# Order of the first four attention groups: scores behind the preceding group's transposes, maxima ahead of its normalisation, fewer fill matmuls

## The chip, the core and the metric

The kernel runs on one core of a Trainium2 chip. The metric is the time of one execution on the device, in microseconds (us). A core has five engines with in-order queues of their own: TensorE (PE in the profile; its weight loads are PEld), VectorE (DVE), ScalarE (ACT), GpSimd (POOL) and SyncE (SP), which here only issues DMA transfers. They wait for each other on semaphores.

## The reference, cut to what matters

A chunked attention with memory keys (4 batches, 8 heads, 768 queries, head size 64) is followed by two pairs of dense layers, all in fp32:

```python
for c in range(nc):                       # chunks of 32 queries
    scores = scale * q_c @ k_full.T       # 8 memory keys and the keys around the chunk
    a = exp(scores - max(scores))
    out_c = (a / (sum(a) + 1e-09)) @ v_full
x = out as (3072 tokens, 512)
h = x @ moe_w_in;  x = (h - tanh(h)) @ moe_w_out         # 512 -> 2048 -> 512
h = x @ moe2_w_in; x = piecewise(h) @ moe2_w_out         # the same sizes
```

The weights arrive as 64-bit floats, as pairs of 32-bit words, and the kernel itself rounds them to fp32.

## The kernel before

**Groups.** The attention is worked in 24 groups of 128 tokens (four chunks of 32). Four groups make one token block of 512, on which the first layer's matmuls run. Groups 0 to 3 are worked alone, ahead of everything else, in the loop `for j in range(PER)` near the end of the kernel; later groups are slipped in between the steps of the layers by tables of events. Instructions stand on each engine in the order in which the Python code issues them: nothing reorders them afterwards.

**One group.** `att_scores` is 64 small matmuls into PSUM (PE). `att_max` is a row maximum and its subtraction (DVE, two instructions of the latter). `att_exp` is one ACT instruction. `att_sum` is a sum, an addition and a reciprocal (DVE). `att_transpose` is 4 transposes of the exponentials (PE), `att_at` copies them to SBUF (ACT), `att_values` is 64 small matmuls with the values (PE), `att_norm` scales by the reciprocal (DVE), `att_x` is 4 transposes (PE). `att_xh` (ACT) and `att_xl` (DVE) split the result into a rounded part xh and a rest xl. Each fp32 product is made of three: xh with whi, xl with whi, xh with wlo.

**Weights.** A 512 KB tile of the first layer (raw_0, raw_1, ... in this text) is brought up in five steps: `round_act` (two ACT instructions), `round_mag` (two on DVE), `round_sign` (one on DVE, one on POOL), `split_weights_hi` (ACT, makes whi) and `split_weights_lo` (DVE, makes wlo). The tile is loaded into one of four staging buffers, so the load of raw_4 waits until POOL is done with raw_0, that of raw_5 for raw_1, and so on.

**The first layer.** `hidden(s)` is one step: 12 matmuls, 4 for each of the parts 0 (xh, whi), 1 (xl, whi) and 2 (xh, wlo). Step 0 is done in two pieces: the columns of groups 0 to 2 (384 columns) inside the loop of the first groups, the rest of group 3 behind it. Two PSUM buffers hold the steps, so `hidden(2)` waits until `gate(0)` (ACT, then DVE) has read step 0, and `hidden(3)` for `gate(1)`.

**Loads.** All of the start's loads stand on SP's queue in a fixed order: queries, keys, then a weight tile, then the values of each group. Each waits for the eighth one before it to land. None of the loads of groups 0 to 3 waits for an engine.

**Fills.** `warm(n, fill)` issues n matmuls on zeros whose result nobody reads. They stand in PE's queue in the pauses of the first groups: 6 behind the scores, 2 behind the transposes, 2 behind the values (`KEEP`).

Of the kernel before, what the change touches and what calls it, by code (L numbers as in the profile page):

```python
# [27 lines left out]
KEYS = NMEM + CTX  # L28
WIN = NMEM + LEFT + CHUNK + SEEN
NPAIR = H // 2  # L30
KC = DM // 128
FC = DFF // 128
NEG = -3.0e38
# [5 lines left out]
PER = 4  # L39
# [3 lines left out]


WARM = 11
KEEP = {"s": 6, "t": 2, "v": 2}

LAG = FC

# [29 lines left out]
def tile_memory_attention_two_mlps(  # L79
# [51 lines left out]
    def round_act(phase, which, fc, part=None, tag=None):  # L131
        stage = stage_t[phase, which, fc]
        low, high = stage[:, :, 0], stage[:, :, 1]
        if part != 1:
            t = slot(tag or (f"raw1_{fc % 3}" if which else f"raw0_{fc}"), f"raw{phase}{which}_{fc}")
            raw_t[phase, which, fc] = t

            nc.scalar.activation(out=t, in_=high.bitcast(F32), func=AF.Abs)
        if part != 0:

            nc.scalar.activation(out=low, in_=low.bitcast(U32), func=AF.Copy, scale=2.0 ** -29)
# [11 lines left out]
    def round_sign(phase, which, fc):  # L153
        stage = stage_t.pop((phase, which, fc))
        bits = raw_t[phase, which, fc].bitcast(I32)
        nc.vector.scalar_tensor_tensor(
            out=bits, in0=stage[:, :, 1], scalar=-0x40000000, in1=bits, op0=ALU.bitwise_and, op1=ALU.bitwise_or
        )

        eng = nc.vector if phase else nc.gpsimd  # L160
        eng.tensor_tensor(out=bits, in0=bits, in1=stage[:, :, 0], op=ALU.add)  # L161
# [7 lines left out]
    def split_weights_hi(s, which):  # L169
        phase, b, fc = steps[s]  # L170
        r = raw_t[phase, which, fc]
        hi = slot(f"whi{which}_{s % (W1O if which else 2)}", f"whi{which}_{s}", F32R)
        nc.scalar.activation(out=hi, in_=r, func=AF.Copy)  # L173
        split_t[s, which] = hi

    def split_weights_lo(s, which):
        phase, b, fc = steps[s]
        r, hi = raw_t[phase, which, fc], split_t[s, which]
        lo = slot(f"wlo{which}_{s % (W1O if which else 2)}", f"wlo{which}_{s}", F32R)
        nc.vector.tensor_tensor(out=lo, in0=r, in1=hi.bitcast(F32), op=ALU.subtract)  # L180
        split_t[s, which] = hi, lo
# [205 lines left out]
    def att_scores(t, pair):  # L387
        qt, kt = st[t]["q"], st[t]["k"]
        sp = pair[:, :, 4 * D:].rearrange("p c (a k) -> p c a k", a=NPAIR)
        for pr in range(NPAIR):  # L390
            for j in range(GC):
                for hh in range(2):
                    nc.tensor.matmul(  # L393
                        sp[j * CHUNK:(j + 1) * CHUNK, hh, pr, :],
                        qt[j][hh * D:(hh + 1) * D, pr, :],
                        kt[j][hh * D:(hh + 1) * D, pr, :],
                        start=True, stop=True,
                    )
        st[t]["sp"] = sp

    def att_max(t):

        e = slots.tile([128, 4, 2, WIN], F32, tag=f"e{t % 2}", name=f"e{t}")
        mx = att.tile([128, 2, NPAIR], F32, tag="mx", name=f"mx{t}")
        s = st[t]["sp"]

        if t % GPB == 0:
            nc.vector.memset(s[:CHUNK, :, :, NMEM:NMEM + LEFT], NEG)
        if t % GPB == GPB - 1:
            nc.vector.memset(s[128 - CHUNK:, :, :, WIN - SEEN:], NEG)  # L410
        nc.vector.tensor_reduce(out=mx, in_=s, op=ALU.max, axis=AX.X)
        st[t]["e"] = e
        if t in BY_HEAD:
            nc.vector.tensor_scalar(out=mx, in0=mx, scalar1=-scale, scalar2=None, op0=ALU.mult)
            st[t]["mx"] = mx
            return
        for hh in range(2):
            nc.vector.tensor_tensor(
                out=e.rearrange("p (b c) u k -> p c u b k", c=2)[:, hh],
                in0=s[:, hh].rearrange("p (u b) k -> p u b k", u=2),  # L420
                in1=mx[:, hh].rearrange("p (u b) -> p u b", u=2)[:, :, :, None].to_broadcast([128, 2, 2, WIN]),
                op=ALU.subtract,
            )

    def att_exp(t):
        e = st[t]["e"]
        if t not in BY_HEAD:
            nc.scalar.activation(out=e, in_=e, func=AF.Exp, scale=scale)
            return
        mx, s = st[t]["mx"], st[t]["sp"]  # L430
        st[t]["r"] = r = att.tile([128, 4, 2], F32, tag="r", name=f"r{t}")
        for g in range(4):
            for u in range(2):
                hh, pr = g % 2, 2 * u + g // 2
                nc.scalar.activation(
                    out=e[:, g, u, :], in_=s[:, hh, pr, :], func=AF.Exp, scale=scale,
                    bias=mx[:, hh, pr:pr + 1], accum_out=r[:, g, u:u + 1],
                )

    def att_sum(t):  # L440
        if t in BY_HEAD:
            r = st[t]["r"]
        else:
            r = att.tile([128, 4, 2], F32, tag="r", name=f"r{t}")
            nc.vector.tensor_reduce(out=r, in_=st[t]["e"], op=ALU.add, axis=AX.X)
        nc.vector.tensor_scalar(out=r, in0=r, scalar1=1e-9, scalar2=None, op0=ALU.add)
        nc.vector.reciprocal(out=r, in_=r)
        st[t]["r"] = r

    def att_transpose(t, p):  # L450
        e = st[t]["e"].rearrange("p g u k -> p g (u k)")
        for g in range(4):
            nc.tensor.transpose(p[:, g * GQ:(g + 1) * GQ], e[:, g, :], ident)  # L453
        st[t]["tp"] = p

    def att_at(t):
        at = slots.tile([128, 4, GQ], F32, tag=f"at{t % 2}", name=f"at{t}")
        nc.scalar.activation(out=at, in_=st[t]["tp"].rearrange("p (g c) -> p g c", g=4), func=AF.Copy)
        st[t]["at"] = at
# [35 lines left out]
    def att_xl(t):  # L495
        b, o = t // PER, t % PER * GQ
        xh, xl = x_tiles(0, b)
        nc.vector.tensor_tensor(  # L498
            out=xl[:, :, o:o + GQ], in0=st.pop(t)["xp"], in1=xh[:, :, o:o + GQ].bitcast(F32), op=ALU.subtract
        )  # L500
# [52 lines left out]
    def hidden(s, n0=0, n1=N, parts=range(3)):  # L553
        phase, b, fc = steps[s]
        xh, xl = x_tiles(phase, b)
        hi, lo = split_t[s, 0]
        if s not in h_t:
            h_t[s] = ps_h.tile([128, 512], F32, tag="h", name=f"h{s}")[:, :N]
        hp = h_t[s][:, n0:n1]
        for j in parts:  # L560
            w, x = ((hi, xh), (hi, xl), (lo, xh))[j]
            for kc in range(KC):
                nc.tensor.matmul(  # L563
                    hp, w[:, kc * 128:(kc + 1) * 128], x[:, kc, n0:n1],
                    start=j == 0 and kc == 0, stop=j == 2 and kc == KC - 1,
                )
# [471 lines left out]
    def warm(n, ps):  # L1038
        for _ in range(n):
            nc.tensor.matmul(ps, zeros[:, :128], zeros, start=True, stop=True)  # L1040
# [9 lines left out]
    load_weights(0, 0, PER - 1)  # L1050
    att_load(PER)

    def start_scores(j):
        pool, tag = ((ps_a, "a"), (ps_acc, "acc0"))[j % 2]
        st_pair[j] = pool.tile([128, 2, 512], F32, tag=tag, name=f"start_a{j}")
        att_scores(j, st_pair[j])

    start_scores(0)
    for j in range(PER):
        last = j == PER - 1  # L1060
        if not last:
            warm(KEEP["s"], fill)
        att_max(j)
        if j:
            att_xl(j - 1)
        if last:
            split_weights_lo(0, 0)
            hidden(0, 0, EARLY_N, (0,))
        if 1 < j:
            round_sign(0, 0, j - 2)  # L1070
        att_exp(j)
        att_sum(j)
        tx = ps_acc.tile([128, 2, 512], F32, tag="acc1", name=f"start_tx{j}")
        att_transpose(j, tx[:, 0, :])
        att_at(j)
        if j == 2:
            split_weights_hi(0, 0)
        if j:
            round_act(0, 0, j - 1)
        if last:  # L1080
            split_weights_hi(1, 0)
            hidden(0, 0, EARLY_N, (1,))
        else:
            warm(KEEP["t"], fill)
        att_values(j, st_pair.pop(j))
        if last:
            hidden(0, 0, EARLY_N, (2,))
        else:
            warm(KEEP["v"], fill)
            start_scores(j + 1)  # L1090
        att_norm(j)
        if last:
            split_weights_lo(1, 0)
        if j:
            round_mag(0, 0, j - 1)
        att_x(j, tx[:, 1, :])
        att_xh(j)
    att_xl(PER - 1)
    round_sign(0, 0, 2)
    round_act(0, 0, 3)  # L1100
    round_rest(0, 0, 3)
    for j in range(AHEAD):
# [105 lines left out]
```

## Time and profile before

| | |
|---|---|
| three runs | 1069.24, 1071.01 and 1071.11 us; median 1071.01 us |
| the profiled execution, first to last instruction | 1070.1 us (0.9 us under the median) |
| PE busy | 1052.4 us, 98% of the span |
| DVE, ACT, POOL busy | 855.7, 650.0 and 42.7 us |
| granted PE clock, mean | 0.997 |

No other time than its span is given for the profiled execution, so sums below are made against 1070.1 us and set on the median. A span counts from the first instruction to the last. "Busy" of PE is near the whole span, so what is left to win or to lose lies in the few stretches in which PE waits; nearly all of them are in the first 60 us, where the changed code stands.

### The profile page before, as it was taken

How to read it: one execution, taken by the hardware profiler on the slowest of the kernel's cores; microseconds unless marked ns; L12 is line 12 of the kernel's file. 1: busy time of each engine (PE TensorE's matmuls, PEld its weight loads, DVE VectorE, ACT ScalarE, POOL GpSimd, SP SyncE). 2: the span in 40 equal slices, each digit the busy share in tenths (PEclk: the TensorE clock that was granted, in tenths of full speed). 3: DMA queues.
4: the chain of work that ended last, by engine and by line, in shares of the span. 5: the costliest groups of instructions: out<-in, count | busy, mean ns of one | idle time of the engine just before them, and what ended most of it. 6: DMA issues, size and time to landing. Idle time of an engine off the chain costs nothing.

```text
span 1070.1 us, 21112 instructions
## 1 busy us (share of the span) xinstructions
PE 1052.4 (98%) x7589; PEld 859.7 (80%) x7589; DVE 855.7 (80%) x1511; ACT 650.0 (61%) x1203; POOL 42.7 (4%) x38
## 2 busy tenths in 40 slices
PE   7799999999999999999999999999999999999998
PEld 3577888888888888888888888888888888888887
DVE  4898987877799999999999778698477787476854
ACT  2687756555455565565566677757477666577553
POOL 0232212000000000000000000000000000000000
PEclk9999999999999999999999999999999999999999
DMA  8999887898889999876487978787766877766774
GB/s 207 245 258 247 260 240 207 258 292 272 266 269 315 325 302 292 292 261 205 154 278 263 313 221 259 210 277 214 232 194 195 261 224 232 214 194 195 203 203 146
DMA packets 212088, 259.37 MB, mean 242 GB/s; under 512 B 65424, under 2 KB 129168, under 8 KB 211984
## 3 DMA queue, kind: packets, MB, share of 16 engines
q1 hardware_dynamic: 211840, 257.88, 80.2%
q8 instruction: 61, 1.00, 0.4%
q14 instruction: 43, 0.35, 0.1%
q10 hardware_dynamic: 144, 0.13, 0.0%
HBM read 199.23 MB, written 58.72 MB: 241 GB/s over the span
## 4 chain that ended last, share of the span: by engine, by line
PE 93%; DMA 2%; SPq 2%; ACT 1%; DVE 1%; issue 0%; ACTq 0%
PE h L563 23%; PE acc L893 21%; PE acc L601 17%; PE qa L805 12%; PE qc L805 6%; PE qb L805 3%; PE acc_-1_1_7132 L893 2%; PE acc_-1_0_7131 L893 2%; DMA stage<-w_in 2%; PE a L467 1%; SPq L364 1%; PE a L393 1%; PE acc_-1_1_7508 L893 1%; PE acc_-1_0_7507 L893 1%; PE b L487 1%; PE b L453 1%
## 5 line engine op out<-in xcount | busy, mean ns | idle before, releaser
L893 PE MATMUL acc<-ghi,inG 128*128 128x512 f32 x672 | 183.0, 389 | 0.0
L576 ACT ACTIVATE g<-h 128x512 f32<-128x512 f32 x96 | 57.7, 601 | 176.7 <-PE h L563 154.9
L893 PEld LDWEIGHTS acc<-ghi,inG 128*128 128x128 f32 x672 | 126.2, 188 | 26.1
L227 DVE TENSOR_TENSOR glo<-g,ghi 128x512 fp32r<-128x512 f32 x174 | 117.8, 688 | 27.4 <-ACT ghi L226 26.3
L805 PE MATMUL qa<-xc,inP 128*128 128x512 f32 x576 | 139.3, 389 | 0.0
L226 ACT ACTIVATE ghi<-g 128x512 fp32r<-128x512 f32 x174 | 107.3, 627 | 43.6 <-DVE glo L227 21.1
L805 PEld LDWEIGHTS qa<-xc,inP 128*128 128x128 f32 x576 | 108.1, 188 | 22.4
L563 PE MATMUL h<-xh,whi 128*128 128x512 f32 (+2 forms) x388 | 105.6, 394 | 3.9 <-DVE g L577 1.9
L893 PE MATMUL acc<-glo,inG 128*128 128x512 f32 x336 | 107.0, 389 | 0.1
L563 PE MATMUL h<-xl,whi 128*128 128x512 f32 (+2 forms) x388 | 104.0, 390 | 0.1
L563 PE MATMUL h<-xh,wlo 128*128 128x512 f32 (+2 forms) x388 | 103.8, 389 | 0.0
L577 DVE TENSOR_TENSOR g<-h,g 128x512 f32<-128x512 f32 x96 | 66.0, 688 | 38.7 <-ACT g L576 38.1
L563 PEld LDWEIGHTS h<-xh,whi 128*128 128x128 f32 x388 | 71.5, 188 | 21.2 <-issue 4.1
L743 ACT ACTIVATE t<-g,half 128x512 f32<-128x512 f32 x72 | 52.2, 725 | 59.1 <-DVE g L739 59.1
L563 PEld LDWEIGHTS h<-xl,whi 128*128 128x128 f32 x388 | 73.0, 189 | 15.2 <-DVE xl L498 0.2
L563 PEld LDWEIGHTS h<-xh,wlo 128*128 128x128 f32 x388 | 72.1, 188 | 14.7
L180 DVE TENSOR_TENSOR wlo<-raw,whi 128x512 fp32r<-128x512 f32 x112 | 80.7, 720 | 0.0
L173 ACT ACTIVATE whi<-raw 128x512 fp32r<-128x512 f32 x112 | 70.5, 630 | 6.5 <-POOL raw L161 6.5
L601 PE MATMUL acc<-ghi,whi 128*128 128x512 f32 x256 | 74.0, 403 | 0.0
L893 PEld LDWEIGHTS acc<-glo,inG 128*128 128x128 f32 x336 | 63.0, 188 | 13.5 <-DVE glo L227 0.5
L805 PE MATMUL qc<-xc,inP 128*128 128x512 f32 x288 | 73.1, 389 | 0.0
L601 PE MATMUL acc<-ghi,wlo 128*128 128x512 f32 x256 | 70.7, 390 | 0.0
(717 smaller groups left out, 1811.3 us busy)
## 6 DMA issues: line engine op xcount, KB each, us to landing
inP<-part SPq DMA_DIRECT2D x168, 256.0 KB, 3.0
inG<-part SPq DMA_DIRECT2D x168, 256.0 KB, 3.0
stage<-w_in SPq DMA_DIRECT2D x32, 512.0 KB, 6.0
stage<-w_out SPq DMA_DIRECT2D x32, 512.0 KB, 5.5
part<-preph SPq DMA_DIRECT2D x64, 256.0 KB, 4.6
whi<-w1o SPq DMA_DIRECT2D x48, 256.0 KB, 4.9
wlo<-w1o SPq DMA_DIRECT2D x48, 256.0 KB, 5.1
part<-prepl SPq DMA_DIRECT2D x48, 256.0 KB, 4.7
```

The source lines that it names most:

```text
L173: nc.scalar.activation(out=hi, in_=r, func=AF.Copy)
L180: nc.vector.tensor_tensor(out=lo, in0=r, in1=hi.bitcast(F32), op=ALU.subtract)
L226: nc.scalar.activation(out=hi, in_=src, func=AF.Copy)
L227: nc.vector.tensor_tensor(out=lo, in0=src, in1=hi.bitcast(F32), op=ALU.subtract)
L364: nc.sync.dma_start(out=k[j // 2][:, j % 2], in_=ks[j, :, :, :WIN])
L563: nc.tensor.matmul(hp, w[:, kc * 128:(kc + 1) * 128], x[:, kc, n0:n1], start=j == 0 and kc == 0, stop=j == 2 and kc == KC - 1,)
L576: nc.scalar.activation(out=g, in_=hp, func=AF.Tanh)
L577: nc.vector.tensor_tensor(out=g, in0=hp, in1=g, op=ALU.subtract)
L601: nc.tensor.matmul(acc_t[dm], w[:, dm * 128:(dm + 1) * 128], g, start=first and j == 0, stop=last and j == 2,)
L743: nc.scalar.activation(out=t, in_=h, func=AF.Relu, scale=0.5, bias=half)
L805: nc.tensor.matmul(o, w[:, k * 128:(k + 1) * 128], z[k], start=i in (1, 2, 5) and j == 0 and k == 0, stop=j == 2 and k == 1, skip_group_ch ...
L893: nc.tensor.matmul(bank[a][c], w[:, c * 128:(c + 1) * 128], g, start=first and j == 0, stop=last and j == 2, skip_group_check=True,)
```

## The change

It rewrites the loop over groups 0 to 3. The scores of group j + 1 now stand on PE right behind the transposes of group j's exponentials, ahead of group j's values. On DVE the maximum and subtraction of group j + 1 stand ahead of the normalisation of group j, and on ACT its exponential ahead of xh of group j. There are 4 fills for each of groups 0 to 2 in place of 10 (12 in place of 30). The work on the weight tiles moves too: raw_0's `round_mag` and `round_sign` stand in the turn of group 2 behind the maximum of group 3, whi_0 and wlo_0 and the first piece of step 0 (parts 0 and 1, then part 2) in the turn of group 3, and whi_1, wlo_1 and the rounding of raw_2 behind the loop. PSUM tiles are named once in place of once for each group. The order of the loads is the same.

```diff
-KEEP = {"s": 6, "t": 2, "v": 2}
+KEEP = 4
...
-    start_scores(0)
+    att_scores(0, start_a[0])
+    att_max(0)
+    att_exp(0)
     for j in range(PER):
         last = j == PER - 1
+        att_transpose(j, start_tx[:, 0, :])
         if not last:
-            warm(KEEP["s"], fill)
-        att_max(j)
-        if j:
-            att_xl(j - 1)
+            att_scores(j + 1, start_a[(j + 1) % 2])
+        att_at(j)
+        att_sum(j)
         if last:
+            split_weights_hi(0, 0)
+            round_mag(0, 0, 1)
             split_weights_lo(0, 0)
-            hidden(0, 0, EARLY_N, (0,))
-        if 1 < j:
-            round_sign(0, 0, j - 2)
-        att_exp(j)
-        att_sum(j)
-        tx = ps_acc.tile([128, 2, 512], F32, tag="acc1", name=f"start_tx{j}")
-        att_transpose(j, tx[:, 0, :])
-        att_at(j)
-        if j == 2:
-            split_weights_hi(0, 0)
-        if j:
-            round_act(0, 0, j - 1)
-        if last:
-            split_weights_hi(1, 0)
-            hidden(0, 0, EARLY_N, (1,))
-        else:
-            warm(KEEP["t"], fill)
-        att_values(j, st_pair.pop(j))
+            hidden(0, 0, EARLY_N, (0, 1))
+            round_sign(0, 0, 1)
+        else:
+            att_max(j + 1)
+        att_values(j, start_a[j % 2])
         if last:
             hidden(0, 0, EARLY_N, (2,))
         else:
-            warm(KEEP["v"], fill)
-            start_scores(j + 1)
+            att_exp(j + 1)
+            warm(KEEP, fill)
         att_norm(j)
-        if last:
-            split_weights_lo(1, 0)
-        if j:
-            round_mag(0, 0, j - 1)
-        att_x(j, tx[:, 1, :])
+        if j == 2:
+            round_mag(0, 0, 0)
+        att_x(j, start_tx[:, 1, :])
         att_xh(j)
-    att_xl(PER - 1)
-    round_sign(0, 0, 2)
+        if 0 < j:
+            round_act(0, 0, j - 1)
+        att_xl(j)
+        if j == 2:
+            round_sign(0, 0, 0)
+    split_weights_hi(1, 0)
+    split_weights_lo(1, 0)
+    round_rest(0, 0, 2)
     round_act(0, 0, 3)
     round_rest(0, 0, 3)
```

Line numbers of the changed kernel are one higher than those of the kernel before in the functions. The first place is PE's queue from the last scores of group 3 to its values, before: start_a is the scores' tile (numbered by group), start_tx the tile of the transposes, h the tile of step 0, raw, whi and wlo the weights with the tile's number in the middle.

```order
L393 MATMUL start_a_529<-starty_163,start_161 32x64 x4
L487 MATMUL start_tx_481<-ident,xn_562 128x128 x4
L563 MATMUL h_579<-xh_354,whi_0_488 128x384 x4
L453 MATMUL start_tx_591<-ident,e_571 128x128 x4
L563 MATMUL h_579<-xl_355,whi_0_488 128x384 x4
L467 MATMUL start_a_529<-starty_164,at_596 32x64 x4
```

And the same place now, from the last fill behind group 2's values:

```order
L1041 MATMUL fill<-zeros 128x512
L488 MATMUL start_tx<-ident,xn_537 128x128 x4
L454 MATMUL start_tx<-ident,e_495 128x128 x4
L564 MATMUL h_568<-xh_354,whi_0_562 128x384 x4
L564 MATMUL h_568<-xl_355,whi_0_562 128x384 x4
L468 MATMUL start_a_223<-starty_164,at_556 32x64 x4
```

In both orders the two blocks of step 0 stand ahead of group 3's values on PE. What moved is what stands between the scores of group 3 and them.

The second place is DVE's queue around the maximum of group 3 (L411, of tile 529; L412 now, of tile 223), before:

```order
L477 TENSOR_TENSOR xn_562<-start_a_420,r_477 128x512
L147 TENSOR_SCALAR raw_1_490<-raw_1_490 128x512
L148 TENSOR_SCALAR raw_1_490<-raw_1_490 128x512
L411 TENSOR_REDUCE mx_572<-start_a_529 128x8
L418 TENSOR_TENSOR e_571<-start_a_529,mx_572 128x2x2x64 x2
L498 TENSOR_TENSOR xl_355<-start_tx_481,xh_354 128x4x128
L180 TENSOR_TENSOR wlo_0_577<-raw_0_381,whi_0_488 128x512
```

And now:

```order
L412 TENSOR_REDUCE mx_496<-start_a_223 128x8
L419 TENSOR_TENSOR e_495<-start_a_223,mx_496 128x2x2x64 x2
L478 TENSOR_TENSOR xn_537<-start_a_222,r_491 128x512
L148 TENSOR_SCALAR raw_0_449<-raw_0_449 128x512
L149 TENSOR_SCALAR raw_0_449<-raw_0_449 128x512
L499 TENSOR_TENSOR xl_355<-start_tx,xh_354 128x4x128
L157 SCALAR_TENSOR_TENSOR raw_0_449<-stage_0_180,raw_0_449 128x512
```

Group 2's normalisation (xn) and the rounding of raw_0 went from ahead of group 3's maximum to behind it. The third place is DVE's queue from group 3's normalisation on, before:

```order
L477 TENSOR_TENSOR xn_643<-start_a_529,r_587 128x512
L180 TENSOR_TENSOR wlo_1_645<-raw_1_490,whi_1_601 128x512
L147 TENSOR_SCALAR raw_2_598<-raw_2_598 128x512
L148 TENSOR_SCALAR raw_2_598<-raw_2_598 128x512
L498 TENSOR_TENSOR xl_355<-start_tx_591,xh_354 128x4x128
L156 SCALAR_TENSOR_TENSOR raw_2_598<-stage_2_202,raw_2_598 128x512
```

And now:

```order
L478 TENSOR_TENSOR xn_615<-start_a_223,r_558 128x512
L499 TENSOR_TENSOR xl_355<-start_tx,xh_354 128x4x128
L181 TENSOR_TENSOR wlo_1_628<-raw_1_546,whi_1_626 128x512
L148 TENSOR_SCALAR raw_2_622<-raw_2_622 128x512
L149 TENSOR_SCALAR raw_2_622<-raw_2_622 128x512
L157 SCALAR_TENSOR_TENSOR raw_2_622<-stage_2_202,raw_2_622 128x512
```

wlo_1 and the first half of raw_2's rounding went from ahead of group 3's xl to behind it. On ACT the making of whi_1 went likewise from ahead of group 3's xh to behind it and behind raw_2's two instructions.

## Rows read from the trace of the kernel before

**Rows 1.** The page's head and its busy times by engine.

```profile
span 1070.1 us, 21112 instructions
...
PE 1052.4 (98%) x7589; PEld 859.7 (80%) x7589; DVE 855.7 (80%) x1511; ACT 650.0 (61%) x1203; POOL 42.7 (4%) x38
```

**Rows 2.** Chain that ended last, in order of time: start, length, what.

```profile
39.99 4.93 DMA stage<-w_in
...
44.94 0.69 ACT raw L138
```

**Rows 3.** PE timeline: start us, us, instructions, [idle before, releaser].

```profile
17.39 1.75 PE L1040 MATMUL fill<-zeros 128*128 128x512 bf16 x6 [2.74 <-issue]
...
29.68 0.76 PE L393 MATMUL start_a<-starty,start 64*32 64x64 f32 x52 [0.43 <-DMA starty<-qkv_t]
...
31.71 1.37 PE L563 MATMUL h<-xh,whi 128*128 128x384 f32 x4 [0.69 <-ACT xh L493]
...
33.58 1.63 PE L563 MATMUL h<-xl,whi 128*128 128x384 f32 x4
...
36.27 0.78 PE L467 MATMUL start_a<-starty,at 64*32 64x64 f32 x54 [0.69 <-DMA starty<-qkv_t]
36.98 0.98 PE L563 MATMUL h<-xh,wlo 128*128 128x384 f32 x4
37.83 0.66 PE L487 MATMUL start_tx<-ident,xn 128*128 128x128 f32 x4
...
49.45 1.15 PE L563 MATMUL h<-xh,whi 128*128 128x512 f32 x4 [1.89 <-DVE g L577]
...
53.95 0.86 PE L467 MATMUL a<-v,at 64*32 64x64 f32 x64 [1.07 <-ACT at L458]
```

**Rows 4.** DVE timeline, the same columns.

```profile
31.20 0.76 DVE L418 TENSOR_TENSOR e<-start_a,mx 128x256 f32<-128x256 f32 x2
...
37.09 0.69 DVE L477 TENSOR_TENSOR xn<-start_a,r 128x512 f32<-128x512 f32 x1 [1.64 <-PE start_a L467]
37.69 0.68 DVE L180 TENSOR_TENSOR wlo<-raw,whi 128x512 fp32r<-128x512 f32 x1
38.29 0.42 DVE L147 TENSOR_SCALAR raw<-raw 128x512 f32<-128x512 f32 x1
...
39.16 0.69 DVE L498 TENSOR_TENSOR xl<-start_tx,xh 128x512 fp32r<-128x512 f32 x1
39.77 0.68 DVE L156 SCALAR_TENSOR_TENSOR raw<-stage,raw 128x512 int32<-128x512 int32 x1
...
42.27 0.69 DVE L156 SCALAR_TENSOR_TENSOR raw<-stage,raw 128x512 int32<-128x512 int32 x1
...
43.48 1.47 DVE L180 TENSOR_TENSOR wlo<-raw,whi 128x512 fp32r<-128x512 f32 x1
45.65 0.43 DVE L147 TENSOR_SCALAR raw<-raw 128x512 f32<-128x512 f32 x1 [0.69 <-ACT raw L138]
```

**Rows 5.** ACT timeline, the same columns.

```profile
38.53 0.60 ACT L493 ACTIVATE xh<-start_tx 128x512 fp32r<-128x512 f32 x1 [2.28 <-PE start_tx L487]
39.02 0.66 ACT L138 ACTIVATE raw<-stage 128x512 f32<-128x512 f32 x1
39.58 0.66 ACT L141 ACTIVATE stage<-stage 128x512 int32<-128x512 uint32 x1
...
41.98 0.64 ACT L173 ACTIVATE whi<-raw 128x512 fp32r<-128x512 f32 x1 [0.33 <-POOL raw L161]
```

**Rows 6.** POOL timeline, the same columns.

```profile
33.88 1.30 POOL L161 TENSOR_TENSOR raw<-raw,stage 128x512 int32<-128x512 int32 x1 [6.38 <-DVE raw L156]
```

**Rows 7.** Windows of 1 us: five engines' busy time, granted clock, DMA share, GB/s.

```profile
33.00:34.00 1.00, 1.00 (x6) 1.00 (x5) 1.00 (x3) 0.00 (x0) 0.12 (x1) 0.50 0.94 222
```

**Rows 8.** SP timeline, the columns of the other timelines.

```profile
39.99 4.77 SPq L126 DMA_DIRECT2D stage<-w_in  x4
```

**Rows 9.** The page's list of DMA issues; its last column is us to landing.

```profile
stage<-w_in SPq DMA_DIRECT2D x32, 512.0 KB, 6.0
```

More of the change, by code (lines that the diff above doesn't have):

```diff
@@ L1051, in tile_memory_attention_two_mlps @@
     att_load(PER)
[L1053 to L1056, printed above, removed]
-    start_scores(0)
+    start_a = [pool.tile([128, 2, 512], F32, tag=tag, name=f"start_a{i}") for i, (pool, tag) in enumerate(((ps_a, "a"), (ps_acc, "acc0")))]
+    start_tx = ps_acc.tile([128, 2, 512], F32, tag="acc1", name="start_tx")
+    att_scores(0, start_a[0])
+    att_max(0)
+    att_exp(0)
     for j in range(PER):
         last = j == PER - 1
+        att_transpose(j, start_tx[:, 0, :])
         if not last:
-            warm(KEEP["s"], fill)
-        att_max(j)
-        if j:
-            att_xl(j - 1)
+            att_scores(j + 1, start_a[(j + 1) % 2])
+        att_at(j)
+        att_sum(j)
         if last:
+            split_weights_hi(0, 0)
+            round_mag(0, 0, 1)
             split_weights_lo(0, 0)
-            hidden(0, 0, EARLY_N, (0,))
-        if 1 < j:
-            round_sign(0, 0, j - 2)
-        att_exp(j)
-        att_sum(j)
-        tx = ps_acc.tile([128, 2, 512], F32, tag="acc1", name=f"start_tx{j}")
-        att_transpose(j, tx[:, 0, :])
-        att_at(j)
-        if j == 2:
-            split_weights_hi(0, 0)
-        if j:
-            round_act(0, 0, j - 1)
-        if last:
-            split_weights_hi(1, 0)
-            hidden(0, 0, EARLY_N, (1,))
-        else:
-            warm(KEEP["t"], fill)
-        att_values(j, st_pair.pop(j))
+            hidden(0, 0, EARLY_N, (0, 1))
+            round_sign(0, 0, 1)
+        else:
+            att_max(j + 1)
+        att_values(j, start_a[j % 2])
         if last:
```

## The prediction

> **What bounds the kernel now.** I read the page's head first: PE is busy for 1052.4 of 1070.1 us [rows 1]. A change in the order of 60 us of work can therefore only win or lose in the 18 us in which PE is idle, and whatever delays PE once it has become the bound is carried to the end unless a later wait swallows it. So I looked for the point from which PE no longer waits, and for what it waited for until then.
>
> The chain of waits has the load of raw_4 in it, from its issue at 39.99 to 44.94 us, and ACT's first look at that tile [rows 2]. Until there the loads set the pace. PE's timeline shows the same from its side [rows 3]. Group 3's scores wait for the keys and resume at 29.68. Group 3's values wait for the values' load and resume at 36.27. Both are landings, and the reader should see that nothing on the engines could have moved them. Behind them stands the last long wait of PE, 1.89 us ahead of step 3 at 49.45, which VectorE ends with gate(1), and one of 1.07 us at 53.95 for ACT. From there on PE is the bound. The time of step 3's start is thus the number to predict: a shift of it is, nearly, the shift of the end.
>
> **The loads.** They stand on SP as before, and those of groups 0 to 3 wait only for each other. So the two landings keep their times, near 29.65 and 36.25. Everything that the change wins in groups 0 to 2 by putting scores and maxima earlier ends at the first of these: group 3's scores end at 29.68 + 0.76 = 30.44, now as before. I cost that gain, and the 18 fills fewer, at nothing: the cover is the wait for the keys. If that cover were gone, the fills would be worth at most the 1.75 us that six of them took at the lower clock [rows 3], three times.
>
> **First term: whi_0 comes late.** Before, raw_0 was rounded ahead of group 3's maximum, and step 0's first block ran at 31.71 [rows 3], in the time that PE had to wait for group 3's values anyway. Now the rounding is queued on DVE behind group 3's maximum, subtraction, and group 2's normalisation, and its last part behind group 2's xl. I follow it by the rows, each instruction at its measured length:
>
> - the subtraction runs at 31.20 as before, to 31.96 [rows 4]
> - group 2's normalisation, 0.69 [rows 4], to 32.65; it could have run at 28, but stands behind the subtraction
> - group 2's att_x on PE, 0.05 later, 0.66 [rows 3], to 33.36; xh on ACT, 0.04 later, 0.60 [rows 5], to 34.00. raw_0's two round_mag instructions, 0.87 from row to row (38.29 to 39.16) [rows 4], lie beside these
> - xl at 34.03; the sign's DVE part 0.61 behind it (39.16 to 39.77) and 0.69 long [rows 4], to 35.33
> - POOL's addition, 1.30 [rows 6], begun 0.1 later, to 36.7; whi_0, 0.64 [rows 5], to 37.4.
>
> Step 0's two blocks can only start at 37.4, and they stand on PE ahead of group 3's values, which landed at 36.25. Here the clock decides. [...] Part 2, the same size, took 0.98 at full clock. In the new order PE has only att_x and the transposes of group 3 to do between 32 and 37.4, with longer pauses than before, so I take the lower level: 3.0 us, to 40.4. Values, 0.86 for 64 matmuls [rows 3], to 41.3. Part 2, 0.98, which hides group 3's normalisation of 0.69, to 42.2. att_x 0.66, xh 0.04 + 0.60: it ends at E = 43.5. Before it ended at 38.53 + 0.60 = 39.13 [rows 5]. **First term: +4.4 us.** At the full clock the two blocks take 2 x 0.98, and the term is +3.4; that is its lower bound. If att_x and the transposes ahead run at the lower clock as well, they lengthen the upper part by about 0.5.
>
> [...]
>
> **Second term: DVE behind xh(3).** Step 3 needs gate(1), which stands on DVE behind raw_2, raw_3, gate(0), wlo_2, raw_4 and group 4's maximum. Before, wlo_1 and raw_2's round_mag ran on DVE while PE and ACT made xh(3), and step 3 began 49.45 - 39.13 = 10.3 us behind E. Now they come behind it, and whi_1 comes behind raw_2's two ACT instructions. From E: these two start 0.11 before E and take 0.56 each from start to start (39.02, 39.58) [rows 5], whi_1 runs from 1.0 to 1.65, and DVE, done with xl at 0.7, waits for it. Then wlo_1 (0.60 to the next row, 37.69 to 38.29), round_mag (0.87): raw_2's sign at 3.2. From raw_2's sign to raw_3's 2.50 (39.77 to 42.27), as before. From there to the end of wlo_2 43.48 + 1.47 - 42.27 = 2.68, so raw_4 at 8.35 [rows 4]. The 0.69 that DVE waited for raw_4 falls away, since its load has long landed. From raw_4's first DVE instruction to step 3 49.45 - 45.65 = 3.80 [rows 3, 4]: step 3 at E + 12.15. **Second term: +1.8 us.** It can be no less than 0.9 (wlo_1 counted, the 1.0 of waiting for whi_1 not), and no more than 2.5 (if the 0.69 stays).
>
> **What else moves.** raw_2 and raw_3 leave POOL later, so the loads of raw_6 and raw_7 (the last two of SP's four from 39.99 to 44.76 [rows 8]), and group 5's loads behind them on SP, are issued some 6 to 7 us later. The load takes 6.0 us [rows 9], the readers move by the two terms too, and in the chain of waits no landing follows raw_4's [rows 2]; I take nothing. The wait of 1.07 at 53.95 hangs on ACT's exponentials of group 4, which start behind the same DVE chain, so it moves along: nothing is swallowed, at most 1.1.
>
> **Sum.** 4.4 + 1.8 = 6.2 us on 1070.1, so 1076.3 for an execution like the profiled one, and on the median, 0.9 higher, 1077.2; I say 1077.0. Bounds: 3.4 + 0.9 - 1.1 = 3.2, or 1074.2; and 4.9 + 2.5 = 7.4, or 1078.4.
>
> **The rivals.**
>
> - *An instruction stall on the path.* Before, PE once stood 2.74 us with no releaser at all ahead of a fill at 17.39 [rows 3]. It cost nothing there, as the loads were behind. The queue is now other in length, and the same stall between 35 and 45 us would cost its full length: 1077.2 + 2.7 = 1079.9. Against it: it is the only one of its size that PE shows.
> - *The late whi_0 costs nothing.* If the keys of group 3 landed 3.1 us sooner, so that the blocks ran by 34.3 and ended by 36.25, the values would still wait for their load, the first term would be nil, and only 1.8 or less is left: 1071 to 1073, no change that can be told. For it: landings vary. Against it: the row's 0.43 us of waiting shows the keys as the last to come, and the same queue issues them.
> - *The loads run ahead, and it is faster.* PE's and DVE's earlier scores and maxima pay if the landings are the ones that move: every us by which SP's whole row of loads runs sooner takes a us off. It decides from 6.2 us on; at 9 us sooner the time would be 1068. For it: the chain has the loads in it until 44.94. Against it: not one of these loads waits for anything that the change touches.
> - *The change does nothing*, since order is decided elsewhere: the queues of the built kernel show that it isn't so.
>
> **How the numbers follow.** Forecast with the lower clock 0.50, with the full clock (1076.2 at +5.2, or less with swallowed waits) 0.20; stall 0.12; costless 0.11; faster 0.07. A measurement can tell about 0.2%, 2.1 us, from no change. Slower by more: 0.50 + 0.20 + 0.12 = 0.82; same 0.11; faster 0.07. The range leaves out the faster case, most of the costless one and the far end of the stall: 1073.0 to 1080.0.
>
> **What would show it.** Group 3's scores should end near 30.4 as before. whi_0 on ACT should end near 37.4, and step 0's first block start there, in place of 31.71; group 3's values should start near 39.4 to 40.4 with ACT or PE ahead of them and no load; xh(3) should end at 42.5 to 43.5. DVE should wait about 1 us for whi_1 behind xl(3), and step 3 should start at about 55.7. If whi_0 is ready before 34.3, the first term is wrong. If step 3 starts 12 us behind xh(3) but the end hasn't moved by as much, later waits have swallowed it. If the keys land at another time than 29.65, the ground under all of it is gone.

## The result and the profile after

The changed kernel takes 1080.03 us, median of four runs (1079.43 to 1082.15). The kernel before, run beside it on the same chip, takes 1070.39 us, median of four (1069.24 to 1071.11). The ratio is 1.0089, 95% interval 1.0068 to 1.0110: slower, as forecast, by 9.6 us where 6.2 had been summed. The forecast of 1077.0 is 3 us short, and the time lies 0.03 us past the upper edge of its range of 1073.0 to 1080.0.

In this run and all later ones the time is 1.7 to 2.0 us above the span, 1.8 in most. The profiled execution of before, of span 1070.1 [rows 1], therefore stands for about 1071.9 us, above its median and not 0.9 below it, as the prediction had put it. The traces differ by 8.1 us and the medians by 9.6; the first profile of before, 1.5 us above its median, makes up the rest.

The head of the page after, as [rows 1]:

```profile
span 1078.2 us, 21069 instructions
...
PE 1054.8 (98%) x7571; PEld 862.9 (80%) x7571; DVE 854.6 (79%) x1511; ACT 649.5 (60%) x1203; POOL 42.6 (4%) x38
```

PE is idle for 5.7 us more, and busy for 2.4 us more although it has 18 fills fewer: the time has gone into its waits and into work at the lower clock (its mean is 0.987 in place of 0.997, and it is 0.50 from 34 to 44 us). Line numbers are one higher than before. PE's timeline, as [rows 3]; row by row these are the rest of group 2's values, group 2's att_x, group 3's transposes, step 0's two blocks, group 3's values, part 2 and att_x, then steps 2 and 3:

```profile
32.45 0.33 PE L468 MATMUL start_a<-start,at 64*32 64x64 f32 x10 [2.29 <-issue]
...
33.60 0.99 PE L488 MATMUL start_tx<-ident,xn 128*128 128x128 f32 x4
36.00 1.11 PE L454 MATMUL start_tx<-ident,e 128*128 128x128 f32 x4 [1.41 <-DVE xl L499]
38.68 1.65 PE L564 MATMUL h<-xh,whi 128*128 128x384 f32 x4 [1.57 <-ACT whi L174]
40.13 1.48 PE L564 MATMUL h<-xl,whi 128*128 128x384 f32 x4
41.54 1.19 PE L468 MATMUL start_a<-starty,at 64*32 64x64 f32 x64
42.66 1.58 PE L564 MATMUL h<-xh,wlo 128*128 128x384 f32 x4
44.07 0.60 PE L488 MATMUL start_tx<-ident,xn 128*128 128x128 f32 x4
...
52.43 1.17 PE L564 MATMUL h<-xh,whi 128*128 128x512 f32 x4 [1.65 <-DVE g L578]
...
57.37 1.79 PE L564 MATMUL h<-xh,whi 128*128 128x512 f32 x4 [1.93 <-DVE g L578]
58.96 1.91 PE L564 MATMUL h<-xl,whi 128*128 128x512 f32 x4
```

The wait for group 3's values' load (0.69 in [rows 3]) is gone. In its place PE waits 1.57 us for whi_0, and before that 1.41 us ahead of group 3's transposes for xl of group 2, which reads the buffer that they write (start_tx). The kernel before has one such buffer too, but there xl of group 2 ran from 31.87 to 32.55 and the transposes at 32.87 did not wait. Two waits for gate(0) and gate(1) stand in front of steps 2 and 3 where there was one. The row with 2.29 has no releaser: PE paused in the middle of group 2's values.

ACT's timeline, as [rows 5], whi_0 and then xh of group 3; POOL's, as [rows 6]; and the window of 1 us, as [rows 7]:

```profile
38.00 0.63 ACT L174 ACTIVATE whi<-raw 128x512 fp32r<-128x512 f32 x1 [0.25 <-POOL raw L162]
...
44.71 0.60 ACT L494 ACTIVATE xh<-start_tx 128x512 fp32r<-128x512 f32 x1 [6.08 <-PE start_tx L488]
```

```profile
36.69 1.28 POOL L162 TENSOR_TENSOR raw<-raw,stage 128x512 int32<-128x512 int32 x1 [35.38 <-DVE raw L157]
```

```profile
39.00:40.00 1.00, 1.00 (x4) 1.00 (x4) 1.00 (x2) 0.00 (x0) 0.00 (x0) 0.50 0.91 225
```

DVE's timeline, as [rows 4]: group 2's normalisation, then behind xh(3) the chain of the second term.

```profile
32.85 0.69 DVE L478 TENSOR_TENSOR xn<-start_a,r 128x512 f32<-128x512 f32 x1 [1.89 <-PE start_a L468]
...
46.96 0.69 DVE L181 TENSOR_TENSOR wlo<-raw,whi 128x512 fp32r<-128x512 f32 x1 [0.93 <-ACT whi L174]
...
48.49 0.69 DVE L157 SCALAR_TENSOR_TENSOR raw<-stage,raw 128x512 int32<-128x512 int32 x1
...
49.55 1.41 DVE L149 TENSOR_SCALAR raw<-raw 128x512 int32<-128x512 int32 x1
...
52.20 1.47 DVE L181 TENSOR_TENSOR wlo<-raw,whi 128x512 fp32r<-128x512 f32 x1
```

The chain of waits, as [rows 2], in order of time (start, length, what). Before, a load stood in it until 44.94. Now it runs through PE's pause, whi_0, step 0's blocks (eight matmuls, 2.93 us), xh(3), and from there through DVE into step 3:

```profile
30.16 2.29 issue
...
38.00 0.64 ACT whi L174
...
38.68 2.93 PE h L564 x8
...
44.71 0.60 ACT xh L494
...
46.96 0.69 DVE wlo L181
...
56.64 0.60 DVE g L578
57.24 0.14 issue
57.37 3.50 PE h L564 x8
```

SP's row of the four weight loads, as [rows 8], is 14.80 us long in place of 4.77, since raw_6 and raw_7 wait for a staging buffer (from 30 to 60 us SP's weight loads wait 13.0 us for POOL); in the 3 us from 46 the DMA share is 0.03:

```profile
38.67 14.80 SPq L127 DMA_DIRECT2D stage<-w_in  x4
```

No landing is in the chain behind them, so this costs nothing here.

### The profile page after: what moved, and what is told of

Same layout as the page of the kernel before. It is cut to its first block, busy times and chain, and to the rows that moved or that the text cites. A ratio compares the mean times of both kernels' runs of the same rounds, so it can differ in the third digit from the quotient of the medians.

```text
span 1078.2 us, 21069 instructions
## 1 busy us (share of the span) xinstructions
PE 1054.8 (98%) x7571; PEld 862.9 (80%) x7571; DVE 854.6 (79%) x1511; ACT 649.5 (60%) x1203; POOL 42.6 (4%) x38
## 4 chain that ended last, share of the span: by engine, by line
PE 92%; DVE 2%; ACT 2%; DMA 1%; SPq 1%; issue 1%; ACTq 0%
PE h L564 22%; PE acc L894 21%; PE acc L602 17%; PE qa L806 12%; PE qc L806 6%; PE qb L806 3%; PE acc_-1_1_7109 L894 2%; PE acc_-1_0_7108 L894 2%; PE a L468 1%; PE a L394 1%; PE acc_-1_1_7485 L894 1%; PE acc_-1_0_7484 L894 1%; ACT e L436 1%; PE b L454 1%; PE b L488 1%
```

## The experiments

All ratios are to the kernel before on the same chip, with 95% intervals; E is the end of xh(3), as in the prediction. E is 39.13 in the profile of before and 45.31 after. The diffs are cut: a call that is put in at a new place is taken out at its old one. None of the first three edits has a ratio clear of the 1.0089 (1.0068 to 1.0110) of the changed kernel; what each does is read from its rows.

**Fills back.** The changed kernel with 30 fills.

```diff
         att_x(j, start_tx[:, 1, :])
+        if not last:
+            warm(6, fill)
```

> The changed kernel with 6 fills more behind att_x of groups 0 to 2, in the pauses in which PE waits for xl: 30 fills again, nothing else. [...] Order theory (the loss is the late whi_0 and DVE's chain behind xh(3), whatever the clock): the span stays within 1 us of 1078.2. [...]

Measured: 1077.57 us, ratio 1.0072 (1.0049 to 1.0094), span 1076.7. Step 0's two blocks:

```profile
39.20 0.97 PE L564 MATMUL h<-xh,whi 128*128 128x384 f32 x4 [2.02 <-ACT whi L174]
40.01 0.87 PE L564 MATMUL h<-xl,whi 128*128 128x384 f32 x4
```

These are their lengths at the full clock (0.95 and 0.86 at a granted 1.00 in order alone; 1.65 and 1.48 at 0.50 in the changed kernel), and from their start to E it is 4.55 us where it was 6.63. So, as an estimate from these two kernels' rows, the lower clock costs the changed kernel 2.1 us there. Fewer fills are only a part of the loss: most of it stays.

**raw_0 early.** Its rounding ahead of group 3's maximum, whi_0 behind group 3's exponential.

```diff
         else:
+            if j == 2:
+                round_mag(0, 0, 0)
+                round_sign(0, 0, 0)
             att_max(j + 1)
...
             att_exp(j + 1)
+            if j == 2:
+                split_weights_hi(0, 0)
```

> The changed kernel with raw_0's round_mag and round_sign ahead of group 3's maximum on DVE and whi_0 behind group 3's exponential on ACT: the weight part of the first term undone. As the changed trace stands, PE waited 1.57 us for whi_0 ahead of step 0's blocks, behind the transposes of group 3, which wait for xl(2) by themselves. My theory: step 0's blocks start right behind those transposes, 1.6 us sooner, span about 1076.6; the rest of the first term stays, as xl(2) is late by the attention's order. Rival (whi_0 is all of the first term): step 0's blocks start at 32 to 34, and the span falls by 4 us or more, to 1074. [...]

Measured: 1077.25 us, ratio 1.0060 (1.0042 to 1.0078), span 1075.5. whi_0 is done at 32.70, and the blocks stand directly behind group 3's transposes at 37.24. But those transposes themselves come only at 36.47, behind xl of group 2:

```profile
36.47 1.12 PE L454 MATMUL start_tx<-ident,e 128*128 128x128 f32 x4 [1.42 <-DVE xl L499]
37.24 1.63 PE L564 MATMUL h<-xh,whi 128*128 128x384 f32 x4
```

E is 42.82, step 3 at 54.88, 12.06 behind it. whi_0 was the last to come, but the blocks start only 1.4 us sooner without it: group 2's turn is late as well. The rest of the 2.5 us by which E is sooner lies in group 3's values and part 2, which took 0.86 and 0.98 here, the lengths before at a granted 1.00, in place of 1.19 and 1.58 at 0.50.

**raw_1 and raw_2 early.** wlo_1 and raw_2's round_mag ahead of xl(3), whi_1 and raw_2's ACT instructions ahead of xh(3), as before the change.

```diff
             round_sign(0, 0, 1)
+            round_act(0, 0, 2)
+            split_weights_hi(1, 0)
...
         att_norm(j)
+        if last:
+            split_weights_lo(1, 0)
+            round_mag(0, 0, 2)
```

> The changed kernel with raw_2's two ACT instructions and whi_1 ahead of xh(3) on ACT, and wlo_1 and raw_2's round_mag ahead of xl(3) on DVE, as before the change: the second term undone alone. My theory: from the end of xh(3) to step 3 10.3 us as before, in place of 12.1, span about 1076.4. Rival (the chain is bound elsewhere, by POOL or by the loads of the staging buffers): step 3 still comes 12 us behind xh(3), span within 0.5 of 1078.2.

Measured: 1076.51 us, ratio 1.0063 (1.0038 to 1.0089), span 1077.1. Step 3 starts at 56.64, 9.55 us behind an E of 47.09, in place of 12.06:

```profile
33.99 0.41 PE L468 MATMUL start_a<-start,at 64*32 64x64 f32 x10 [3.07 <-issue]
...
56.64 1.17 PE L564 MATMUL h<-xh,whi 128*128 128x512 f32 x4 [1.12 <-DVE g L578]
```

The second term is confirmed at 2.5 us. In the profiled execution, the longest of four, longer pauses of PE (1.72 and 3.07 us, in place of 1.16 and 2.29) hid half of it.

**Weights late alone.** The kernel before with its own attention and 30 fills, the weights' work placed as in the change.

```diff
         att_max(j)
+        if last:
+            round_mag(0, 0, 0)
         if j:
             att_xl(j - 1)
         if last:
-            split_weights_lo(0, 0)
-            hidden(0, 0, EARLY_N, (0,))
-        if 1 < j:
-            round_sign(0, 0, j - 2)
+            round_sign(0, 0, 0)
...
     att_xl(PER - 1)
-    round_sign(0, 0, 2)
+    split_weights_hi(1, 0)
+    split_weights_lo(1, 0)
+    round_rest(0, 0, 2)
```

> The kernel before, with its attention order and its 30 fills, and the weights' work where the change puts it: raw_0 rounded behind group 3's maximum, whi_0, wlo_0 and step 0's first piece behind at(3), whi_1, wlo_1 and raw_2 behind the loop. My theory: both terms appear, the first smaller since xl(2) is not late: whi_0 at about 36.2, xh(3) ends at 41.4 to 42.4 (+2.3 to +3.3), step 3 12.1 us behind it (+1.8), span 1074.2 to 1075.2. Rival (the attention's order and the fills make the loss): at most +1.8, span up to 1071.9.

Measured: 1075.45 us, ratio 1.0053 (1.0035 to 1.0071), span 1074.4. The blocks wait 1.97 us for whi_0 and take 1.65 and 1.48 us, as in the changed kernel at 0.50, though there are 30 fills; E is 41.08 and step 3 starts 12.08 behind it:

```profile
34.55 1.65 PE L563 MATMUL h<-xh,whi 128*128 128x384 f32 x4 [1.97 <-ACT whi L173]
36.00 1.48 PE L563 MATMUL h<-xl,whi 128*128 128x384 f32 x4
...
53.16 1.89 PE L563 MATMUL h<-xh,whi 128*128 128x512 f32 x4 [1.95 <-DVE g L577]
```

whi_0 was done at 34.50, 1.7 us sooner than I expected. Both terms of the prediction stand in this kernel by themselves, and give a little over half of the loss.

**Weights back.** The changed kernel with both edits, raw_0 early and raw_1 and raw_2 early.

> The changed kernel with both weight parts undone: raw_0 rounded ahead of group 3's maximum with whi_0 behind group 3's exponential, and whi_1, wlo_1 and raw_2's first half ahead of xh(3) and xl(3). The attention's order and the 12 fills of the change stay. My theory (two terms from the weights' work, 4.3 us in the run that has them alone, and the rest from the attention's order, the clock and stalls): xh(3) ends near 42.8, step 3 comes 9.6 to 10.3 behind it, span 1073.0 to 1074.0. Rival (the weights' work is the whole loss): span within 1 us of 1070.1.

Measured: 1074.46 us, ratio 1.0044 (1.0031 to 1.0058), span 1072.9. About half the loss is left. One piece of the weights' work is still late here: raw_1 is rounded in group 3's turn, while the kernel before has its `round_mag` in group 2's turn and its `round_sign` ahead of group 3's exponential. In this profile nothing on PE waits for it (xh(3), at 42.08, waits for PE), so the half that is left is the attention's own order, the fills and PE's pause.

**Fewer fills alone.** The kernel before with `KEEP = {"s": 2, "t": 1, "v": 1}`, 12 fills.

> The kernel before with 12 fills in place of 30 (2 behind the scores, 1 behind the transposes, 1 behind the values), all else as before. [...]

Measured: 1071.92 us (1068.91 to 1075.11, ten runs), ratio 1.0022 (1.0009 to 1.0036). I had expected next to nothing (a span within 0.8 us of 1070.1), and was wrong: in the order of before the 18 fills are worth some 2.4 us (1.0 to 3.8). The profiled execution (span 1069.0, where the ten reach from 1067.1 to 1073.3) doesn't show the loss: its step 1 began at the lower clock (at 40.67, its first block 2.02 us long; granted 0.56 in the 3 us from 40), but ahead of step 3 PE then didn't wait. Where the others lose it stays open.

**Group 3 behind group 2.** The changed kernel with group 3's scores, maximum and exponential behind the whole turn of group 2.

```diff
         if j == 2:
             round_sign(0, 0, 0)
+            att_scores(3, start_a[1])
+            att_max(3)
+            att_exp(3)
```

> The changed kernel with the boundary between groups 2 and 3 undone: group 3's scores, maximum and exponential stand behind the whole turn of group 2 (with raw_0's rounding in it); groups 0 to 2, weights behind and fills as changed. My theory (group 2's normalisation and with it xl(2) and raw_0 are late because they stand behind group 3's scores and maximum): whi_0 at about 35.2 in place of 38.0, step 0's blocks from about 35.3, step 3 12.1 us behind xh(3) as changed, span 1074.5 to 1075.5. Rival (the order of scores and maxima costs nothing, only whi_0's own place does): span within 1 us of 1078.2, as group 3's exponentials are some 3 us later.

Measured: 1080.42 us, ratio 1.0095 (1.0080 to 1.0110), span 1078.9. No gain; my expectation failed. raw_0's rounding is no longer behind group 3's maximum, but whi_0 is now behind group 3's exponential and copy on ACT, and comes at 39.25 in place of 38.00:

```profile
36.87 0.63 ACT L429 ACTIVATE e<-e 128x512 f32<-128x512 f32 x1 [1.68 <-DVE e L419]
38.75 0.60 ACT L459 ACTIVATE at<-start_tx 128x512 f32<-128x512 f32 x1 [1.26 <-PE start_tx L454]
39.25 0.62 ACT L174 ACTIVATE whi<-raw 128x512 fp32r<-128x512 f32 x1
```

One queue was cleared and the other took its place.

**The pause moved by 12 matmuls.** The changed kernel with `WARM = 7` and fills for group 2 alone.

> The changed kernel with 12 fills fewer ahead of group 2's values (7 in place of 11 at the start, none in the turns of groups 0 and 1). PE's waits that nothing releases stood at its recorded matmul 222 before, and at 350 and 478 after, 128 apart. Theory that they belong to a place in the instruction stream: with 12 matmuls fewer ahead, matmul 478 is no more in group 2's values but behind them, in the fills or group 2's att_x; the values run through in 0.9 to 1.2 us, and the normalisation of group 2 follows group 3's subtraction at once, up to 2 us sooner, if the stall isn't as long there. Rival (they come by time, when PE is fast or the loads are thick): the values of group 2 are broken again for 1 to 3 us. The span by the first 1076.5 to 1078.5, as the clock may be low for longer; by the second 1078 to 1079.

Measured: 1079.07 us, ratio 1.0081 (1.0064 to 1.0098), span 1077.8. Group 2's values now run through, and the pause stands 12 matmuls later in the program, between the second and the third fill behind them:

```profile
32.45 0.61 PE L1041 MATMUL fill<-zeros 128*128 128x512 bf16 x2 [2.31 <-issue]
```

It still holds up att_x of group 2, which stands behind it on PE, so little is won.

**Order alone.** Weights back and 30 fills: of the change the attention's order is left, and raw_1's later place.

> The changed kernel with the weights' work back at its earlier places (as in the run before the last ones) and with 30 fills again, so that of the change only the attention's own order is left. Theory (the fewer fills cost about 0.2% by themselves, by the lower clock that the thinly used PE is granted): ratio to the kernel before near 1.002 (1.001 to 1.0035), step 0's two blocks at 0.97 and 0.87 us in place of 1.63 and 1.48, step 3 one to two us earlier than the 52.23 of the run with 12 fills. Rival (the rest is the order of the attention and the pause of PE in group 2's values, 2.08 us, which the fills do not touch): ratio 1.0035 or more, span 1072 to 1073.5.

Measured: 1074.12 us, ratio 1.0041 (1.0024 to 1.0057), span 1071.8. The ratio is the rival's, though its interval reaches into the theory's range: beside weights back (1.0044), the fills give nothing that can be told from zero. In its profile the blocks take 0.95 and 0.86 (granted clock 1.00 from 34 to 37), and E is 39.09 where weights back has 42.68. But whi_1 has to wait for raw_1, xh(3) stands behind whi_1 on ACT and xl(3) behind raw_2's rounding on DVE, and then the clock falls for steps 0 and 1 (0.59 in the 3 us from 40, 0.50 in those from 43):

```profile
37.97 0.63 ACT L174 ACTIVATE whi<-raw 128x512 fp32r<-128x512 f32 x1 [1.97 <-POOL raw L162]
38.51 0.58 ACT L494 ACTIVATE xh<-start_tx 128x512 fp32r<-128x512 f32 x1
```

```profile
39.14 0.66 PE L564 MATMUL h<-xh,whi 128*128 128x128 f32 x4 [1.29 <-ACT xh L494]
40.78 1.12 PE L564 MATMUL h<-xl,whi 128*128 128x128 f32 x4 [0.98 <-DVE xl L499]
...
42.55 2.02 PE L564 MATMUL h<-xh,whi 128*128 128x512 f32 x4
```

Step 3 starts at 51.32, 12.23 us behind E in place of 9.55. So most of what the fills won ahead of E was lost behind it, and the 0.41% is not the price of the order by itself.

**The pause moved to a wait.** Weights back, `WARM = 1`, fills for group 2 alone: 18 matmuls fewer than with the weights back.

> As the run with the weights' work back (span 1072.9, ratio 1.0044), but 1 matmul in place of 11 ahead of the first scores and fills for group 2 alone, which makes 18 matmuls fewer ahead of group 3's transposes. Theory (PE's pause without releaser sits at a fixed count of matmuls, here 18 matmuls later in the program, at group 3's transposes, where PE waits 1.4 us for xl of group 2 anyway): group 2's values run through, xl of group 2 is done near 33.7 in place of 35.7, and the span falls to 1070.8 to 1071.5. Rival (the pause belongs to the place, or the lower clock of a PE with 8 fills fewer takes back what it gives): the span stays within 0.8 us of 1072.9.

Measured: 1072.44 us, ratio 1.0029 (1.0018 to 1.0040), span 1071.4. No pause is left in the profile, group 3's transposes run at 33.05 in place of 35.77, and E is near 38.6. This is in the theory's span. The intervals of the two ratios overlap, so the 1.5 us are shown by the rows more than by the times. Behind E step 1 runs at the lower clock, as in order alone (its first block, at 42.03, takes 2.02 us; the clock is 0.52 in the 3 us from 40 and 0.50 in those from 43), which takes back a part of the 2.7 us.

```profile
33.05 0.65 PE L454 MATMUL start_tx<-ident,e 128*128 128x128 f32 x4 [1.41 <-DVE xl L499]
```

**Gate first.** An attempt to beat both: the kernel before, with group 4's maximum and gate(1) ahead of raw_4's rounding, and group 4's exponentials ahead of raw_5's.

```diff
+        if i == 0:
+            hidden(1, 0)
+            run(between, 0)
+            gate(1)
+        if i == 1:
+            rounds[1] = [e for e in rounds[1] if e[1] is not slot_exp or e[1](*e[2])]
         run(before, i)
         run(rounds, i)
```

> The kernel before, with its first groups untouched; only behind step 1 the maximum of group 4 and gate(1) stand ahead of the rounding of raw_4, and the exponentials of group 4 ahead of that of raw_5. Theory (PE's wait of 1.89 us at step 3 and that of 1.07 us ahead of group 4's values are waits for DVE's and ACT's queue order, not for data): step 3 starts near 47.6 in place of 49.45, the time is 1.5 to 2.5 us less, ratio 0.9976 to 0.9987. Rival (the weights of steps 4 and 5, rounded 1 to 2 us later, become the next wait, at about 53 to 58 us): ratio 0.9995 to 1.001, with PE waiting for wlo or whi there.

Measured: 1069.74 us, ratio 1.0002 (0.9993 to 1.0010). Step 3 no longer waits (45.23), but the wait ahead of group 4's values is 2.38 in place of 1.07 us:

```profile
50.96 0.86 PE L467 MATMUL a<-v,at 64*32 64x64 f32 x64 [2.38 <-ACT at L458]
```

**Copy first.** The same, with ACT's copy of group 4's transposes ahead of whi_4 and raw_6.

```diff
+        if i == 2:
+            hidden(3, parts=(0, 1))
+            run(inside, 2)
         if 0 <= i <= LAST:
             split(i + 2)
```

> The run with gate(1) first moved PE's wait from step 3 (1.89 us) to group 4's values (1.07 to 2.38 us), where ACT's copy of group 4's transposes stood at 50.27 behind the tanh of step 2, whi of tile 4 and the two instructions on raw_6. This kernel adds to it that the copy stands ahead of whi_4 and raw_6. Theory (ACT's order is what PE waits for there, and steps 4 and 5 have slack): group 4's values start about 1.6 us sooner than with gate(1) first, 2 to 2.5 us sooner, counted from the end of xh of group 3, than in the kernel before (14.8 us), and the time is 1.5 to 2.5 us less: ratio 0.9977 to 0.9987. Rival (whi_4 or wlo_4 is then what step 4 waits for, or a lower clock takes it back): ratio 0.9993 to 1.001, with PE waiting at step 4 or at group 5.

Measured: 1070.17 us, ratio 1.0005 (0.9996 to 1.0014). Group 4's values start 11.65 us behind an E of 36.80, where it was 14.82; that wait is gone. Others have come, for DVE above all:

```profile
49.82 1.16 PE L563 MATMUL h<-xh,whi 128*128 128x512 f32 x4 [0.51 <-DVE g L577]
...
53.83 0.86 PE L393 MATMUL a<-k,q 64*32 64x64 f32 x64 [1.01 <-DVE xn L477]
...
58.28 1.16 PE L563 MATMUL h<-xh,whi 128*128 128x512 f32 x4 [0.64 <-DVE g L577]
```

DVE's busy time in the 27 us from 40 is 25.34 us in the kernel before and 26.02 here. So I take DVE's work, and not the order, for the limit behind E; no run with less work on DVE tests this. Neither attempt beats the kernel before.

These two kernels have the first groups of before unchanged, and E at 36.90 and 36.80, not 39.13: group 3's values ran through from 33.44 in the one and resumed at 33.88 in the other, where they resumed at 36.27 in [rows 3]:

```profile
33.44 0.97 PE L467 MATMUL start_a<-starty,at 64*32 64x64 f32 x64
```

```profile
33.88 0.78 PE L467 MATMUL start_a<-starty,at 64*32 64x64 f32 x54 [0.21 <-DMA starty<-qkv_t]
```

The landings of the kernel before thus vary by more than 2 us, and the execution profiled first was a late one.

## Why the prediction was right in its sign and short by 3 us

**Landings.** They did not keep their times: group 3's scores were done at about 29.4, not at 30.44, and waited for no load. This gained nothing, since PE's pause came behind it. By its own last sign (keys at another time than 29.65) the prediction had lost its ground; that the first term still came near is in part luck, as the pause took back what the earlier keys gave. The step "I cost that gain, and the 18 fills fewer, at nothing" was wrong. With the weights back and 30 fills the new order still costs 0.41% (0.24 to 0.57), a number that has raw_1's later place in it; no run takes that out alone. The rows point to the cause: group 2's values, ahead of group 3's scores before, now stand on PE behind them, so group 2's normalisation, att_x, xh and xl, and group 3's transposes behind them, all come later (33.05 us even with no pause, against 32.03 with the gate first). In order alone ACT's copy for the values was done at 27.89 and they began at 29.05, since the weight loads of the scores ahead of them waited 0.98 us for keys. In the changed kernel's own trace they began 0.26 us behind the copy, and what held them was the pause. No run gives the transposes a second buffer, which would show what their wait for xl is worth. In the prediction all this was inside the chain to whi_0, where the one late whi_0 seemed to pay for all of it.

**First term.** Predicted 4.4 us, and 6.2 in the trace. The mechanism was right: whi_0 ended at 38.63 (37.4 predicted), the blocks ran at a granted 0.50 in 2.93 us (3.0 predicted: the 1.37 and 1.63 of [rows 3], with 0.50 from 33 to 34 [rows 7]), and the load was no longer waited for. Two sizes were off. whi_0 was 1.2 us late: 0.9 because PE's pause of 2.29 us delayed group 2's normalisation to 32.85 (31.96), and 0.3 because att_x ran at a lower clock (0.99 in place of 0.66; granted 0.89 from 33 to 34, 0.50 from 34 on). And the 0.50 held on to 44: values at 1.19 (0.86) and part 2 at 1.58 (0.98) took 2.5 us from row to row in place of 1.8.

**Second term.** Predicted step 3 at E + 12.15, measured 12.06 after, with the fills back and with raw_0 early too, and 9.55 with whi_1, wlo_1 and raw_2's work moved back. That is 2.5 less, about the 1.8 predicted and the 0.69 that the kernel before spent waiting for raw_4. DVE's wait for whi_1 is 0.93 (predicted about 1). This was the step that held best, and the two last runs speak for why: DVE is nearly full from E on (25.15 and 26.02 of the 27 us from 40), so work put behind E is paid in full. The prediction had PE as the bound from step 3 on; the two runs took PE's waits there away, and others came in their place.

**Swallowed.** The wait of 1.07 at 53.95 [rows 3] is gone after, as the bound of 1.1 allowed, but steps at the lower clock (1.79 and 1.91, at 0.50 from 58 to 60, against 1.15 for the first in [rows 3]) took it back: step 3 is 7.9 us later than before, the end 8.1.

**The rivals.** The stall did come on the path, from 30.16 to 32.45 and not between 35 and 45; its 1079.9 is nearest to the time, by a sum of other terms. A late whi_0 without cost, loads that pay, and a change without effect are ruled out by the chain.

**The sum.** From 6.2 to the 9.6 us measured: the first term is 1.8 larger, the second 0.1 smaller, 0.2 comes behind step 3, which makes the traces' 8.1, and 1.5 is the late first profile of before. That the two traces came within 2 us of the 6.2 is in part the luck of that profile. By the runs, weights late alone give 0.53% and order with fewer fills 0.44%; together 0.97%, against 0.89 (0.68 to 1.10) measured, with raw_1's later place in both. So about half of the loss is the two terms, and about half is what I costed at nothing: the new order, the fills and PE's pause, which the runs don't split further.

## What to carry to other kernels

When a change sends work earlier on one in-order queue, write down what it overtakes: scores that waited for a load held up values that had all they needed (by 1.2 us in order alone). Undo each half of a change alone, since one late operand at the end of a chain can look like the whole price. And before removing a wait, look at how full the engine behind it is: with DVE busy for 25 of 27 us, two reorderings took away 3 us of waits and gained nothing that can be told.

## What the runs showed of the hardware that was not expected

In these rows PE pauses without a releaser, and where it does, it is at the same counts of its matmuls. Counted along PE's queue, in the whole traces before and after and in the other runs from 24 us on at the latest (copy first from 30), every such pause of over 1 us stands ahead of matmul 222 (before, 2.74 us [rows 3]), 349 or 350 (seven runs, 1.16 to 2.94 us) or 478 (five runs, 1.33 to 3.07 us), that is 128 apart, whatever stands there: fill, scores or values. From the first of the changed kernel's two pauses to the second, its rows have 128 matmuls and 127 weight loads. Not every such place has a pause: with the fills back and in order alone the 478th runs through. Put on a place where PE waits for DVE (1.41 us for xl at 33.05, the pause moved to a wait), the pause is not seen. Gate first, from 22 us on, and copy first show none. What causes the pause no run shows.

Twice in the rows after, DVE's instructions took 1.41 and 1.47 us in place of 0.43 and 0.68: both began during one of POOL's additions (49.31 to 50.67 and 51.82 to 53.12) and ended 0.29 and 0.55 us behind it. What held them no run shows.

The clock fell to 0.50 also with 30 fills ([rows 7]; order alone, in the 3 us from 43), and in weights late alone the blocks at 34.55 took 1.65 and 1.48 us, as in the changed kernel at 0.50. So the number of fills did not decide it. PE had waited just before, 0.69 us [rows 3], 0.98 and 1.97; but a wait alone did not decide it either, since with the fills back PE waited 2.02 us ahead of 39.20, and the blocks took 0.97 and 0.87, near the 0.95 and 0.86 that they took in order alone at 1.00.
